# The first of three block pairs with eight plain d_ff tiles, and GpSimd's sums moved to VectorE

## The chip, the cores and the metric

The kernel runs on one core of one Trainium2 chip. Its time is the device time of one execution in microseconds. TensorE multiplies, VectorE, ScalarE and GpSimd work on elements, and SyncE here only sends transfers between the chip's outer memory (DRAM) and SBUF, the memory that the engines work in. Each engine runs its instructions in order. TensorE writes to PSUM, which has eight banks of 128 x 512 floats here. TensorE's clock has two levels, 1.2 and 2.4 GHz; the profile's column PEclk shows the mean share of the upper one that was granted.

## The reference

Attention with a memory (B = 4, H = 8, S = 576, D = 64) gives x, 2304 tokens of 512 numbers. A gated network follows, with d_ff = 1536:

```
g   = x @ w_gate                    # 2304 x 1536
u   = g * sigmoid(g) * (x @ w_val)
out = u @ w_out                     # 2304 x 512
```

The change concerns this second part alone. Weights come as 64-bit floats and are rebuilt as 32-bit ones on the chip.

## The kernel before, in words

**Precision.** A number is held as a high and a low part in TensorE's type; a product of two such numbers is three matmuls (high-high, high-low, low-high). Making the parts is a copy on ScalarE (the high one) and a subtraction on VectorE (the low one).

**Stages.** The attention runs first. Beside it d_ff tiles 0 to 3 (of twelve, 128 wide) are finished for tokens 0 to 1535, with their sums in the DRAM tensor `part`. x goes to the DRAM tensors `xdh` and `xdl`. Then comes the stage that the change is about, from line 693 on. It goes over three block pairs of 2 x 384 tokens in the order 1536, 0, 768 (`ORDER`): block pair 1 does all twelve tiles, pairs 2 and 3 do tiles 4 to 11 and add `part`.

**A unit** is one d_ff tile of one block pair. There are two ways to do its products with w_gate and w_val:

- *plain*, `eight` (L890): eight block products of the 2 x 2 split (2 token blocks, 2 halves of d_model, gate and value): 48 matmuls of 384 columns;
- *seven products*, `seven` (L918): a scheme with seven block products (`p1` to `p7`): 42 matmuls. It needs sums of weight blocks (`operands`, L744) and of x blocks (`fetch`, L788, and `sums`, L810), all of them split into parts again (`mixed`, L802, for x).

The gate goes through Silu on ScalarE, VectorE multiplies by the value (L909, L938), `halves` (L879) splits the result. The sums into d_model (`lower`, L858) are 18 matmuls of 512 columns for a unit; they stand between the products of the next unit. `inline` (L832) fixes this order on TensorE. The products use two PSUM banks in turn (`bank`, L886); the other six hold the output of a block pair.

Before, the first four units (tiles 0 to 3 of block pair 1) are plain and all others take seven products.

**Weights.** `weights2` (L708) converts one tile in three steps (gate, value, out), each with a load of 512 KB into one of two `wrawb` buffers (L711), L714 on ScalarE and L715, L721 and L722 on VectorE. Tiles 4 to 7 (`keep`) have buffers of their own, as plain floats for gate and value, from which `operands` makes both kinds of parts. Tiles 8 to 11 take over the buffers of tiles 0 to 3, as parts (`wsplit`); for them `operands` adds the parts together first, on GpSimd (L750). `convert` (L740) emits as many steps at each unit as `PACE` says: four at each of the first four, then one, then two. They go in the order of tiles 4 to 11.

**x.** `direct` (L798) loads parts of x from DRAM as they are (p1, p2, p4; for the plain units also p7). `fetch` loads the four blocks of a pair, the high parts into `xr` and the low parts, one after another, into the single buffer `xt`, and adds them on GpSimd (L795, 768 columns each). `sums` makes four sums of them on GpSimd (L804). `tokens` (L821) does both for the next block pair after the last unit of one.

**What sets the order.** Within an engine the order is fixed when the program is built: a planner takes instructions by a priority, which is the order of emission unless `later_by(n)` moves it n places back, and by times that it estimates. All loads of this stage go through SyncE's one queue.

Of the kernel before, what the change touches and what calls it, by code (L numbers as in the profile page):

```python
# [19 lines left out]
NPAIR = H // 2  # L20
# [25 lines left out]
PACE = (4, 4, 4, 4, 1, 1, 1, 1, 2, 2)  # L46
# [17 lines left out]
def attention_moe(ctx: ExitStack, tc: tile.TileContext, qt, kt_, v, m, beta, wg, wv, wo, out):  # L64
# [630 lines left out]
    with tc.tile_pool(name="w2", bufs=1, reuse_waits="tile") as w2, \  # L695
# [38 lines left out]
        def more():  # L734
            for f in later:
                yield from weights2(f)
# [51 lines left out]
        def fetch(t0):  # L788

            got = rot(mbp, "xr", [128, 4, 2, N2], F32, 1)  # L790
            for n, (i, j) in enumerate(((1, 0), (1, 1), (0, 0), (0, 1))):
                tmp = rot(mbp, "xt", [128, 2, N2], F32, 1)
                SP.dma_start(got[:, n], block(xdh, t0, i, j))
                SP.dma_start(tmp, block(xdl, t0, i, j))
                POOL.tensor_tensor(got[:, n], got[:, n], tmp, op=ALU.add)  # L795
            return got

        def direct(t0, p, i, j):  # L798
            for dst, src in zip(xs[p], (xdh, xdl)):
                SP.dma_start(dst.bitcast(F32), block(src, t0, i, j))  # L800

        def mixed(got, p, out, a, b, op):  # L802

            POOL.tensor_tensor(out, a, b, op=op)  # L804
# [5 lines left out]
        def sums(got, which):  # L810
            a21, a22, a11, a12 = (got[:, n] for n in range(4))
            if "p6" in which:
                s = rot(mbp, "xm", [128, 2, N2], F32, 1)
                s1 = rot(mbp, "xt", [128, 2, N2], F32, 1)
                mixed(got, "p5", s1, a21, a22, ALU.add)
                mixed(got, "p6", s, s1, a11, ALU.subtract)
                mixed(got, "p3", a12, a12, s, ALU.subtract)
            if "p7" in which:
                mixed(got, "p7", a11, a11, a21, ALU.subtract)

        def tokens(t0, got):  # L821
            direct(t0, "p1", 0, 0)
            direct(t0, "p2", 0, 1)
            direct(t0, "p4", 1, 1)
            sums(got, ("p6", "p7"))

        blocks = [(t0, later if t0 < NT1 else list(range(NF))) for t0 in ORDER]
# [62 lines left out]
        def eight(f, down):  # L890

            hi, lo = wsplit[f]
            u = []
            for i, at in enumerate((("p1", "p2"), ("p7", "p4"))):
                g = hold(("zg", "zh")[i])
                for gv in range(2):
                    ps = bank()
                    n = 0
                    for kk in range(NPAIR):
                        o = gv * 512 + (kk + 2 * gv) % 4 * 128  # L900
                        c = slice(o, o + 128)
                        xh, xl = (x[:, kk % 2, :] for x in xs[at[kk // 2]])
                        for wt, xx in ((hi, xh), (hi, xl), (lo, xh)):
                            inline(PE.matmul(ps[:, 0:N2], wt[:, c], xx, start=(n == 0), stop=(n == 11)))
                            n += 1
                    if gv == 0:
                        ACT.activation(g, ps[:, 0:N2], AF.Silu, scale=W_ONE)
                    else:
                        DVE.scalar_tensor_tensor(  # L909
                            out=g, in0=ps[:, 0:N2], scalar=W_ONE, in1=g, op0=ALU.mult, op1=ALU.mult  # L910
                        )
                        u.append(halves(i, g))
                    if down and (i or gv):
                        for _ in range(2):
                            down.pop(0)()
# [27 lines left out]
        for p, i, j in (("p1", 0, 0), ("p2", 0, 1), ("p7", 1, 0), ("p4", 1, 1)):  # L943
            direct(first, p, i, j)
        ready = {}
        last = None
        for n, unit in enumerate(units):
            t0, f, fs = unit
            whole = f not in keep and n < FC1
# [5 lines left out]
            if FC1 - 1 <= n < len(units) - 1:  # L955
                with later_by(LATE):
                    ready[n + 1] = operands(units[n + 1][1])
            if f == fs[-1] and t0 != blocks[-1][0]:
# [3 lines left out]
                lambda j=j, last=last: lower(*last, j) for j in (range(2 * nj) if n <= FC1 else TURN)  # L962
            ]
            last = (unit, eight(f, down) if whole else seven(ready.pop(n), down))
            if n == FC1 - 1:
                sums(got, ("p7",))
            if f == fs[len(fs) // 2] and t0 != blocks[-1][0]:
                got = fetch(blocks[[t for t, _ in blocks].index(t0) + 1][0])
            if f == fs[-1] and t0 != blocks[-1][0]:
                tokens(units[n + 1][0], got)  # L970
            if f == fs[1] and t0 == blocks[-1][0]:
                whole_x = got.rearrange("p n k c -> p (n k c)")
# [54 lines left out]
```

## Time and profile before

| | us |
|---|---|
| median of 3 runs | 759.21 |
| lowest and highest | 754.63, 762.9 |
| the profiled execution | 761.55 |
| its span, first to last instruction | 759.5 |
| start of the first plain unit in it | 370.93 |

The profile is of one execution. Its instructions are named by engine (PE is TensorE, DVE VectorE, ACT ScalarE, POOL GpSimd, SP SyncE; PEld the loading of weights into TensorE), by line, and by tile as output<-inputs. Times of the trace count from the first instruction. A row of busy time gives a stretch from:to, its length, then for PE, PEld, DVE, ACT and POOL the busy us and (x how many instructions), then PEclk, the share of time that the DMA engines were busy, and GB/s. A busy engine is one with an instruction under way, whatever that instruction itself waits for.

### The profile page before, as it was taken

Reading aid. Unit: us, or ns where it says so; the run is one execution under the profiler, and the core shown is the slowest. Engines: PE = TensorE matmul, PEld = TensorE weight load, DVE = VectorE, ACT = ScalarE, POOL = GpSimd, SP = SyncE. Lnnn points to the kernel's source line nnn. Section 1 sums busy time; section 2 is a strip of 40 time slices with the busy share of each in tenths; the row PEclk is TensorE's granted clock in tenths of the full one; section 3 lists DMA queues with packets and bytes.
Section 4 is the critical chain, followed back from the end, with each engine's and each line's share of the span. In section 5 each row is a group of like instructions: output and inputs, shape, how many; then the busy total and the mean of one; then the engine's idle time right before and its main releaser. Section 6 shows DMA issues by size and latency. Waiting matters only on the chain.

```text
span 759.5 us, 11605 instructions
## 1 busy us (share of the span) xinstructions
PE 685.0 (90%) x4028; PEld 603.8 (80%) x4028; DVE 559.2 (74%) x1298; ACT 416.7 (55%) x909; POOL 271.8 (36%) x288
## 2 busy tenths in 40 slices
PE   5798989999899998999889585979997999999998
PEld 3586769997798977988778574858986999989996
DVE  8999736867877778776469979996678765874544
ACT  6667538586666866757434353553473343643431
POOL 5998545443555435522014325112015320002100
PEclk9999899999899998999979897999999899999999
DMA  9455452303623124020484552320164000620002
GB/s 260 165 170 183 134 163 69 113 13 108 196 86 84 48 97 160 33 100 6 143 303 156 188 187 69 121 83 1 54 196 139 29 0 1 194 98 1 0 1 83
DMA packets 49562, 80.45 MB, mean 106 GB/s; under 512 B 12256, under 2 KB 30176, under 8 KB 49504
## 3 DMA queue, kind: packets, MB, share of 16 engines
q1 hardware_dynamic: 49360, 79.42, 32.4%
q8 instruction: 31, 0.51, 0.3%
q10 hardware_dynamic: 144, 0.29, 0.1%
q14 instruction: 27, 0.22, 0.1%
HBM read 62.40 MB, written 17.30 MB: 105 GB/s over the span
## 4 chain that ended last, share of the span: by engine, by line
PE 56%; DVE 23%; DMA 8%; issue 5%; ACT 5%; POOL 3%; SPq 0%; DVEq 0%; ACTq 0%; POOLq 0%
PE g L844 9%; PE m L844 9%; PE tr L865 5%; PE s L865 4%; PE g L207 4%; PE s L406 3%; PE m L207 3%; PE tr L483 3%; PE av L626 2%; PE av L865 2%; DMA wrawb<-in_wg_dram 2%; PE av L612 2%; DMA wrawb<-in_wv_dram 1%; PE m L216 1%; DVE wab L722 1%
## 5 line engine op out<-in xcount | busy, mean ns | idle before, releaser
L750 POOL TENSOR_TENSOR rb<-wh,wl 128x1024 f32<-128x1024 f32 x12 | 30.2, 2513 | 151.5 <-DVE tt L768 138.1
L770 DVE TENSOR_TENSOR tl<-tt,th 128x512 fp32r<-128x512 f32 x48 | 36.1, 752 | 40.7 <-ACT th L769 40.6
L795 POOL TENSOR_TENSOR xr<-xr,xt 128x768 f32<-128x768 f32 x12 | 23.1, 1929 | 117.4 <-DMA xt<-xdl 103.8
L769 ACT CAST th<-tt 128x512 fp32r<-128x512 f32 x48 | 29.8, 621 | 60.1 <-PE m L844 29.4
L420 ACT ACTIVATE pl<-pl,mx 128x384 f32<-128x384 f32 (+1 forms) x64 | 42.5, 666 | 26.0 <-DVE mx L416 25.9
L459 POOL TENSOR_SCALAR pl<-pl,rs 128x384 f32<-128x384 f32 (+1 forms) x64 | 45.7, 732 | 18.5 <-ACT x L510 12.2
L114 DVE TENSOR_TENSOR g2l<-tr,g2h 128x512 fp32r<-128x512 f32 (+1 forms) x66 | 36.6, 572 | 19.7 <-ACT g2h L465 19.1
L459 POOL TENSOR_SCALAR ps<-ps,rs 128x128 f32<-128x128 f32 (+1 forms) x64 | 28.2, 460 | 55.5 <-DVE rs L456 36.1
L483 PE MATMUL tr<-ident,pl 128*128 128x128 f32 x224 | 39.9, 310 | 6.6 <-POOL pl L459 4.2
L416 DVE CUSTOM_DVE_ANT_0 pl<-s,maskp 128x384 f32<-128x384 f32 (+1 forms) x56 | 33.0, 618 | 13.1 <-PE s L406 13.0
L406 PE MATMUL s<-kh,qh 64*128 64x128 f32 (+3 forms) x112 | 26.1, 443 | 15.9 <-DVE mx L416 9.1
L483 PEld LDWEIGHTS tr<-ident,pl 128*128 128x128 f32 x224 | 28.8, 158 | 13.1 <-POOL pl L459 7.6
L465 ACT CAST g2h<-tr 128x512 fp32r<-128x512 f32 (+1 forms) x66 | 31.0, 493 | 10.5 <-PE tr L483 9.9
L420 ACT ACTIVATE ps<-ps,mx 128x128 f32<-128x128 f32 (+1 forms) x64 | 28.8, 451 | 8.1 <-DVE mx L416 8.0
L406 PEld LDWEIGHTS s<-kh,qh 64*128 64x128 f32 x112 | 11.8, 198 | 24.7 <-DVE mx L416 10.8
L510 ACT COPY x<-av 64x256 f32<-64x256 f32 (+1 forms) x44 | 17.3, 394 | 25.1 <-PE av L626 15.3
L626 PE MATMUL av<-g2h,vs 128*128 128x320 f32 (+2 forms) x110 | 30.1, 289 | 0.1
L714 ACT ACTIVATE web<-wrawb 128x512 f32<-128x512 f32 x24 | 16.1, 673 | 24.6 <-DMA wrawb<-in_wg_dram 11.1
L626 PE MATMUL av<-g2l,vs 128*128 128x320 f32 (+2 forms) x110 | 29.4, 300 | 0.2
L511 DVE TENSOR_TENSOR x<-av,x 64x256 f32<-64x256 f32 (+1 forms) x44 | 19.9, 453 | 12.8 <-ACT x L510 12.2
L110 POOL TENSOR_SCALAR qh<-qr 128x640 fp32r<-128x640 f32 x16 | 12.7, 794 | 43.9 <-PE s L437 40.5
L882 ACT CAST uh<-zh 128x384 fp32r<-128x384 f32 x28 | 14.3, 512 | 23.8 <-DVE zh L938 12.5
(405 smaller groups left out, 2655.1 us busy)
## 6 DMA issues: line engine op xcount, KB each, us to landing
qr<-in_qt_dram SPq DMA_DIRECT2D x16, 384.0 KB, 4.0
xr<-xdh SPq DMA_DIRECT2D x12, 384.0 KB, 4.2
xt<-xdl SPq DMA_DIRECT2D x12, 384.0 KB, 4.2
kr<-in_kt_dram SPq DMA_DIRECT2D x15, 288.0 KB, 3.5
xdh<-xh SPq DMA_DIRECT2D x15, 288.0 KB, 2.4
xdl<-xl SPq DMA_DIRECT2D x15, 288.0 KB, 3.2
wrawb<-in_wg_dram SPq DMA_DIRECT2D x8, 512.0 KB, 3.7
wrawb<-in_wv_dram SPq DMA_DIRECT2D x8, 512.0 KB, 3.5
```

Source lines behind the costliest of these rows:

```text
L114: return eng.tensor_tensor(dst, src, hi.bitcast(F32), op=ALU.subtract)
L207: PE.matmul(ps, wt[:, c], xx[:, kk, :], start=(n == 0), stop=(n == 11))
L406: mm = PE.matmul(ps[h][:, 0:w], q[rows, t * 128 : t * 128 + 128], k[rows, 0:w], start=(i == 0), stop=(i == 2))
L416: read[id(ps[h])] = DVE.tensor_tensor_reduce(out=p[:, 0:w], in0=ps[h][:, 0:w], in1=maskp[:, 512 - w : 512], op0=ALU.add, op1=ALU.min, scal ...
L420: ACT.activation(p[:, 0:w], p[:, 0:w], AF.Exp, bias=mx[:, c + h : c + h + 1], scale=-1.0, accum_out=self.sm[:, c + h : c + h + 1],)
L459: POOL.tensor_scalar(p, p, rs[:, i : i + 1], 1.0, op0=ALU.mult, op1=ALU.mult)
L465: ACT.copy(view(g[0]), src)
L483: PE.transpose(tr[:, c * 128 : c * 128 + 128], p[:, (k0 + c) * 128 : (k0 + c) * 128 + 128], ident)
L626: PE.matmul(av[:, o:320], self.vs[:, h, kk, :], keys, start=(kk == 0 and g is self.g2[0]), stop=(kk == 4 and g is self.g2[1]),)
L770: DVE.tensor_tensor(tl[:, c], t[:, c], th[:, c].bitcast(F32), op=ALU.subtract)
L844: inline(PE.matmul(ps[:, 0:N2], wt[:, c], xx[:, kk, :], start=(start and n == 0), stop=(n == 5), skip_group_check=not start,))
L865: inline(PE.matmul(po[j], a[:, c], b, start=(f == fs[0] and n == 0), stop=(f == fs[-1] and n == 2)))
```

## The change

- In block pair 1 the tiles go in the order 0 to 3, 8 to 11, 4 to 7. The first eight are plain, the last four take seven products. The other pairs are as before.
- Tiles are converted in the order 4, 5, 8, 9, 10, 11, 6, 7 (`TURNS`), three steps (one tile) at each of the eight plain units.
- The sums that GpSimd made (L750 as two halves of 512 columns, L795, L804) are on VectorE.
- `mixed` is taken apart: `sums` makes all four sums of a pair at one place, `spread` splits one of them.
- `fetch` and `sums` for the next block pair are emitted at the fourth and third unit from a pair's end, behind by `LATE` = 60 places; for the first pair at units 1 and 2, with the splits at units 3, 4, 5 and 7.
- `direct` loads each half of a block's d_model (k) with a transfer of its own, and for the first pair in the order p1, p7, then p2 and p4 by k.
- In the first unit (`begin`) the four products are made together, half of d_model by half, with two of the output's banks beside the two of the ring, so that p1 and p7 come first. In the last plain unit (`back`) the second token block goes first.

The core of the diff:

```
-PACE = (4, 4, 4, 4, 1, 1, 1, 1, 2, 2)
+TURNS = (4, 5, 8, 9, 10, 11, 6, 7)
...
-                POOL.tensor_tensor(w, bh[:, 0:1024].bitcast(F32), bl[:, 0:1024].bitcast(F32), op=ALU.add)
+                for c in (slice(0, 512), slice(512, 1024)):
+                    DVE.tensor_tensor(w[:, c], bh[:, c].bitcast(F32), bl[:, c].bitcast(F32), op=ALU.add)
...
-                POOL.tensor_tensor(got[:, n], got[:, n], tmp, op=ALU.add)
+                DVE.tensor_tensor(got[:, n], got[:, n], tmp, op=ALU.add)
...
+        def direct(t0, p, i, j, ks=(0, 1)):
+            for k in ks:
+                for dst, src in zip(xs[p], (xdh, xdl)):
+                    SP.dma_start(dst[:, k].bitcast(F32), block(src, t0, i, j)[:, k])
...
+            DVE.tensor_tensor(s1, a21, a22, op=ALU.add)
+            DVE.tensor_tensor(s, s1, a11, op=ALU.subtract)
+            DVE.tensor_tensor(a12, a12, s, op=ALU.subtract)
+            DVE.tensor_tensor(a11, a11, a21, op=ALU.subtract)
+            return dict(p6=s, p7=a11, p5=s1, p3=a12)
+
+        def spread(mix, p):
             h, l = xs[p]
             for k in range(2):
-                ACT.copy(h[:, k], out[:, k])
-                DVE.tensor_tensor(l[:, k], out[:, k], h[:, k].bitcast(F32), op=ALU.subtract)
+                ACT.copy(h[:, k], mix[p][:, k])
+                DVE.tensor_tensor(l[:, k], mix[p][:, k], h[:, k].bitcast(F32), op=ALU.subtract)
...
+        whole = list(range(FC1)) + later[NF - 2 * FC1 :]
+        blocks = [(t0, later if t0 < NT1 else whole + later[: NF - 2 * FC1]) for t0 in ORDER]
...
+        def eight(f, down, begin, back):
...
+            if begin:
+                for ks in ((0, 1), (2,)):
+                    for i, gv in todo:
+                        run(i, gv, ks)
+            for i, gv in todo:
+                ps = run(i, gv, (3,) if begin else range(NPAIR))
...
+        direct(first, "p1", 0, 0)
+        direct(first, "p7", 1, 0)
+        for k in range(2):
+            direct(first, "p2", 0, 1, (k,))
+            direct(first, "p4", 1, 1, (k,))
...
             with later_by(LATE):
-                convert(PACE[n] if n < len(PACE) else 0)
-            if n == 1:
-                got = fetch(first)
-                sums(got, ("p6",))
+                if n < nw:
+                    convert(3)
+                if n == 1:
+                    got = fetch(first)
+                if n == 2:
+                    mix = sums(got)
+                if 3 <= n < 6:
+                    spread(mix, ("p6", "p5", "p3")[n - 3])
...
+            if n < nw:
+                last = (unit, eight(f, down, n == 0, n == nw - 1))
+            else:
+                last = (unit, seven(ready.pop(n), down))
+            if n == nw - 1:
+                spread(mix, "p7")
+            if not end:
+                follows = blocks[[t for t, _ in blocks].index(t0) + 1][0]
+                with later_by(LATE):
+                    if at == len(fs) - 4:
+                        got = fetch(follows)
+                    if at == len(fs) - 3:
+                        mix = sums(got)
+                if at == len(fs) - 1:
+                    tokens(follows, mix)
```

## Rows read from the trace of the kernel before

**Rows 1.** Page, part 1: busy us (share of the span) and instructions of each engine

```profile
PE 685.0 (90%) x4028; PEld 603.8 (80%) x4028; DVE 559.2 (74%) x1298; ACT 416.7 (55%) x909; POOL 271.8 (36%) x288
```

**Rows 2.** Busy time (length; PE, PEld, DVE, ACT, POOL; clock): units, then block pair 1

```profile
370.93:390.24 19.31, 13.95 (x61) 12.43 (x60) 6.02 (x13) 6.05 (x10) 0.00 (x0) 0.73 0.83 284
390.24:402.76 12.52, 12.52 (x68) 11.72 (x67) 11.68 (x20) 5.95 (x11) 4.07 (x2) 1.00 0.55 194
416.20:438.85 22.65, 14.61 (x67) 13.49 (x66) 20.03 (x31) 6.97 (x14) 8.05 (x4) 0.85 0.57 178
455.89:478.90 23.01, 14.70 (x61) 12.85 (x60) 21.55 (x28) 8.33 (x17) 10.73 (x6) 0.78 0.25 85
478.90:522.23 43.33, 37.06 (x181) 31.29 (x180) 40.97 (x76) 23.57 (x46) 7.72 (x3) 1.00 0.22 74
522.23:533.71 11.48, 11.48 (x61) 10.66 (x60) 6.35 (x14) 4.67 (x10) 2.60 (x1) 1.00 0.00 0
370.93:556.67 185.74, 153.64 (x738) 137.40 (x738) 148.51 (x250) 84.25 (x163) 44.40 (x21) 0.92 0.40 134
```

**Rows 3.** Busy time by stretch: block pair 2, its longest unit, block pair 3

```profile
556.67:657.38 100.71, 95.46 (x481) 87.61 (x480) 71.20 (x121) 47.46 (x96) 25.42 (x12) 0.97 0.25 76
580.63:599.98 19.35, 14.82 (x61) 13.09 (x60) 16.80 (x17) 5.37 (x12) 11.27 (x6) 0.82 0.13 41
657.38:751.11 93.73, 92.38 (x481) 84.92 (x479) 51.66 (x103) 37.00 (x74) 7.60 (x3) 1.00 0.11 38
```

**Rows 4.** TensorE in order of time: start, us, instruction, [idle before <-releaser]

```profile
426.48 0.69 PE L904 MATMUL g<-xbh,wh 128*128 128x384 f32 x1 [8.04 <-DVE zh L909]
```

**Rows 5.** VectorE in order of time, ahead of that L909

```profile
420.67 2.28 DVE L722 SCALAR_TENSOR_TENSOR wr<-wrawb,wr 128x512 int32<-128x512 int32 x1
422.88 0.41 DVE L715 TENSOR_SCALAR web<-web 128x512 f32<-128x512 f32 x1
...
424.13 0.69 DVE L722 SCALAR_TENSOR_TENSOR wr<-wrawb,wr 128x512 int32<-128x512 int32 x1
424.73 0.55 DVE L808 TENSOR_TENSOR xp5l<-xt,xp5h 128x384 fp32r<-128x384 f32 x1
425.20 0.42 DVE L760 TENSOR_TENSOR tt<-wr 128x256 f32<-128x256 f32 x1
```

**Rows 6.** GpSimd in order of time: the last of four sums in a row

```profile
420.29 2.11 POOL L804 TENSOR_TENSOR xr<-xr 128x768 f32<-128x768 f32 x1
```

**Rows 7.** L770 (ns min/median/max, first and last start); a wait of block pair 1 (us, times, longest)

```profile
L770 DVE TENSOR_TENSOR tl<-tt,th x48: 677/693/2310, 394.6 to 726.4; 128x512 fp32r<-128x512 f32 x48
...
DVE web L715 <- ACT web L714: 14.5, 9, 7.3
```

**Rows 8.** Page, part 5: GpSimd's L750 and L795, busy, mean ns | idle before, releaser

```profile
L750 POOL TENSOR_TENSOR rb<-wh,wl 128x1024 f32<-128x1024 f32 x12 | 30.2, 2513 | 151.5 <-DVE tt L768 138.1
...
L795 POOL TENSOR_TENSOR xr<-xr,xt 128x768 f32<-128x768 f32 x12 | 23.1, 1929 | 117.4 <-DMA xt<-xdl 103.8
```

**Rows 9.** SyncE in order of time, around the start of block pair 1

```profile
370.36 0.41 SPq L253 DMA_DIRECT2D part<-o  x1
...
376.87 0.32 SPq L640 DMA_DIRECT2D xdl<-xl  x1
377.29 0.40 SPq L800 DMA_DIRECT2D xp7h<-xdh  x1
```

**Rows 10.** TensorE in order of time, the first plain unit

```profile
380.91 0.66 PE L904 MATMUL m<-xp7h,wh 128*128 128x384 f32 x1 [3.56 <-DMA xp7h<-xdh]
...
382.64 0.52 PE L904 MATMUL m<-xp7h,wl 128*128 128x384 f32 x1
382.96 0.52 PE L904 MATMUL m<-xp7h,wh 128*128 128x384 f32 x1
```

**Rows 11.** Page, part 6: loads, KB each, median us from issue to landing

```profile
xt<-xdl SPq DMA_DIRECT2D x12, 384.0 KB, 4.2
...
wrawb<-in_wg_dram SPq DMA_DIRECT2D x8, 512.0 KB, 3.7
```

More of the change, by code (lines that the diff above doesn't have):

```diff
@@ L734, in more @@
         def more():
-            for f in later:
+            for f in TURNS:
                 yield from weights2(f)
@@ L888, in bank @@
             return ring[turn2[0] % 2]
-        def eight(f, down):
+        def eight(f, down, begin, back):
             hi, lo = wsplit[f]
[L893 to L915, printed above, removed]
@@ new lines, in eight, with run @@
+            u = [None, None]
+            todo = [(i, gv) for i in ((1, 0) if back else (0, 1)) for gv in range(2)]
+            held = {}
+            def run(i, gv, ks):
+                if (i, gv) not in held:
+                    held[(i, gv)] = po[2 * nj - 2 + gv] if begin and i else bank()
+                ps = held[(i, gv)]
+                for kk in ks:
+                    o = gv * 512 + (kk + 2 * gv) % 4 * 128
+                    c = slice(o, o + 128)
+                    at = (("p1", "p2"), ("p7", "p4"))[i][kk // 2]
+                    xh, xl = (x[:, kk % 2, :] for x in xs[at])
+                    for n, (wt, xx) in enumerate(((hi, xh), (hi, xl), (lo, xh))):
+                        inline(PE.matmul(
+                            ps[:, 0:N2], wt[:, c], xx, start=(kk == 0 and n == 0), stop=(kk == NPAIR - 1 and n == 2)
+                        ))
+                return ps[:, 0:N2]
@@ new lines, in eight @@
+            if begin:
[4 more added lines that the diff above has]
+                ps = run(i, gv, (3,) if begin else range(NPAIR))
+                if gv == 0:
+                    g = hold(("zg", "zh")[i])
+                    ACT.activation(g, ps, AF.Silu, scale=W_ONE)
+                else:
+                    DVE.scalar_tensor_tensor(out=g, in0=ps, scalar=W_ONE, in1=g, op0=ALU.mult, op1=ALU.mult)
+                    u[i] = halves(i, g)
+                if down and (i, gv) != todo[0]:
+                    for _ in range(2):
+                        down.pop(0)()
@@ L948, in attention_moe @@
             t0, f, fs = unit
[L949 removed]
+            at = fs.index(f)
+            end = t0 == blocks[-1][0]
             with later_by(LATE):
[L951 to L956 removed]
+                if n < nw:
[6 more added lines that the diff above has]
+                    spread(mix, ("p6", "p5", "p3")[n - 3])
+                if nw - 1 <= n < len(units) - 1:
                     ready[n + 1] = operands(units[n + 1][1])
[L958 removed]
+            if at == len(fs) - 1 and not end:
                 for j in TURN[0:nj]:
@@ L961, in attention_moe @@
             down = [] if last is None else [
-                lambda j=j, last=last: lower(*last, j) for j in (range(2 * nj) if n <= FC1 else TURN)
+                lambda j=j, last=last: lower(*last, j) for j in (range(2 * nj) if n <= nw else TURN)
             ]
[L964 to L972, printed above, removed]
+            if n < nw:
+                last = (unit, eight(f, down, n == 0, n == nw - 1))
+            else:
+                last = (unit, seven(ready.pop(n), down))
[10 more added lines that the diff above has]
+                    tokens(follows, mix)
+            if at == 1 and end:
+                whole_x = slots["xr"][1][0].rearrange("p n k c -> p (n k c)")
                 for j in range(2 * nj):
```

31 lines of the change are left out of this document (10 added, 21 removed).

## The prediction

> **What bounds the kernel now.** I read the page first, then the busy time unit by unit (a unit is one d_ff tile of one block pair, its products on TensorE and the sums into d_model of the unit before it), then single instructions where a unit is long. The page shows TensorE busy for 90% of the span and VectorE for 74%; GpSimd has 271.8 us [rows 1]. That average hides two regimes. In block pair 1 (from 370.93 us) a plain unit takes 12.52 us and a seven-product unit 11.48 us when TensorE never waits [rows 2]: the difference, 1.04 us, is six matmuls of 384 columns. Four plain and eight seven-product units need 4 x 12.52 + 8 x 11.48 = 141.9 us; the block took 185.74. In block pair 2, 8 x 11.48 = 91.84 stands against 100.71, in block pair 3 against 93.73 [rows 3]. So block 1 loses 43.8 us, block 2 8.9, block 3 1.9, and the product work itself is the floor.
>
> What ends the waits is read at the longest one. TensorE stands 8.04 us before a matmul that needs a PSUM bank which VectorE's L909 has to read [rows 4]. Ahead of L909 in VectorE's order stand instructions of 2.1 to 2.3 us; the same line, L722, takes 0.69 us a little later [rows 5]. The long ones stand while GpSimd runs its sums of the experts' inputs back to back, the last at 420.29 for 2.11 us, and the short ones begin when it is through [rows 6]. So here an engine that is off the critical path lengthens VectorE's instructions to its own two microseconds, by about 1.5 us each (2.28 instead of 0.69). Block 1 has 21 GpSimd operations [rows 2], so some 21 x 1.5 = 31 us of VectorE's 148.5 busy us are this lengthening; VectorE is busy for 80% of the block.
>
> **The change, part by part.** All durations are of the profiled run, from instructions that nothing lengthened: VectorE takes 0.42 us for 256 columns, 0.55 for 384, 0.42 for a one-operand 512 and 0.69 for L722 [rows 5], and 0.69 for 512 columns with two SBUF operands [rows 7].
>
> 1. *Plain products.* Units of tiles 8 to 11 in block 1 become plain: 4 x 1.04 = +4.2 us of TensorE. The floor of block 1 is 8 x 12.52 + 4 x 11.48 = 146.1 us, less what unit 0 doesn't have (below). Their operands (L750, then 3.1 us of VectorE each) fall away, and with them the chain conversion, GpSimd sum, VectorE sums that the late seven-product units waited for: three such units take 43.33 us, 3.0 us each above 11.48, with VectorE busy for 40.97 of them [rows 2].
>
> 2. *GpSimd's sums go to VectorE.* L750 (12 now, 8 after), L795 (12) and L804 (12) leave GpSimd [rows 8]. A 768-column add on VectorE isn't in the trace. It costs more than a 512-column one (0.69) and less than two of them (1.38); these three sizes rise by 0.14 per 128 columns, so I take 0.69 + 0.28 = 0.97 us. The two halves of L750 are 1.38 us. VectorE gets 24 x 0.97 + 8 x 1.38 = 34 us over the span, 15.5 of it in block 1 (the 16 adds of two fetches and their sums; all operands made there are of tiles 4 to 7), and loses about 31 us of lengthening in block 1 alone.
>
> 3. *Does VectorE then have room?* A plain unit's own work is 4 x 0.55 = 2.2 us. A tile's conversion is three times 0.42 + 0.42 + 0.69 and one or three subtractions of 0.69: 5.3 us (tiles 4 to 7) or 6.7 (8 to 11). With a fetch (3.9), sums (3.9), one expert's split (1.1) and operands (4.2) where they fall, units 0 to 7 hold 7.5, 11.4, 12.7, 10.0, 10.0, 10.0, 7.5, 12.7: 82 us against about 105 of products. A seven-product unit's own work is 7 x 0.55 = 3.9 us, operands 4.2 (4.4 with L750's halves). Units 8, 9 and 11 come to 11.9, 11.9 and 12.4 of 11.48, and so do four more at the later block boundaries; the others to some 8. In the rows, the instruction behind L722 starts 0.60 us after it, and L722 shows 0.69 [rows 5], so these sums are high by a tenth. VectorE has room, with seven tight units.
>
> 4. *The start.* Unit 0 takes 19.31 us now at a mean clock of 0.73 [rows 2]. SyncE, in order, sends p7's loads at 377.29, behind the last attention pair's store at 376.87 [rows 9]; the first product on p7 waits 3.56 us and then runs 0.52 us a matmul instead of 0.34 [rows 10]. The change asks for p7 before p2 and p4, and takes products as data come. At best p7 leaves in the queue's free time after 370.36 [rows 9], and only the last pair's columns are late: stored by about 379, loaded some 4 us later [rows 11], end near 383, so 12 us. At worst p7 again leaves at 377, now with 12 products to do before it and not 24, and 36 products follow at the lower of the two clock levels: 380.9 + 27 x 0.32 (the steps in [rows 10]) + 9 x 0.17 = 391, so 20 us. The order of SyncE's queue decides, which this trace can't show; I take 17, nearer the worst, since the queue now has p7 behind that store. The 20 DMA issues more that the split by k brings cost SyncE 0.4 us each, in a queue that is mostly free.
>
> 5. *Order of conversions.* Three per unit instead of four and then one; tiles 8 to 11 are ready two units ahead. Each unit needs three loads of 512 KB at 3.7 us [rows 11] in 12.5 us, through two buffers: covered, but the adds of a fetch share SyncE's queue and its one xt buffer. Where the conversion is late, L715 stands at the head of VectorE's queue and L909 behind it. I take 2 us for units 1 to 7 (bounds 0 and 10: now unit 1 loses nothing and unit 3, with GpSimd's sums inside, 10.1 [rows 2]).
>
> 6. *What remains as stall.* Units 8 to 11: 2 us; block 2: 2; block 3: 2 as now. Bounds: 0, and for each of the seven tight units the 3.0 us that the three crowded units lose [rows 2].
>
> **The sum.** Block 1: 17 + 7 x 12.52 + 2 + 4 x 11.48 + 2 = 154.6 instead of 185.7: -31.1. Block 2: 91.84 + 2 = 93.8 instead of 100.7: -6.9. Block 3 and the tail behind it: 0. Together -38.0 us. The profiled execution took 761.55 us (span 759.5), which gives 723.5; its time lies 2.3 us above the median of the runs, from which it gives 721.2. I say 722 us.
>
> **Rivals.**
> *VectorE becomes the bound.* The seven tight units each lose 3.0 us, 20.7 instead of the 6 that parts 3 and 6 allow: +15, so 737 us. For: their sums exceed 11.48 us, and a seven-product unit gives VectorE less time per bank than a plain one. Against: in block 2 as it is, most units run without a wait and VectorE has 29 us free [rows 3], and the background work may slide over a unit. The Trainium skill, page "Perfetto Trace Analysis", section "Optimizing Scalar/DVE Operations", speaks for this rival: with DVE saturated, offloading to GPSIMD may make sense, and the change does the opposite. By that sentence alone block 1 would grow by the 15.5 us moved; the same section doubts the offload between these two, because they share a read port, and the lengthened rows agree with the doubt.
>
> *Everything hides.* Unit 0 at 12 us, no stall but block 3's 1.9: 723.5 - 5 - 6 = 712.5, and 711 off the median.
>
> *The stalls are the loads', not GpSimd's.* VectorE waited 14.5 us for L714 in block 1, which waits for weight loads [rows 7], and some stalls come with GpSimd idle. If only the stalls of the three units with GpSimd's sums go (10.1, 11.5 and 7.9 us [rows 2, 3]) and 4.2 us of products are added: 761.5 - 29.5 + 4.2 = 736. If none go: 766, which is no change.
>
> *Slower: the adds stand at the head of VectorE's queue.* GpSimd spent 117.4 us idle before the 12 adds of L795, 103.8 of it for the landing of xt [rows 8]: 9.8 us each. GpSimd held up nobody by that. VectorE runs in order, and an add that waits there holds L909, L928 and every split behind it; TensorE is covered, by the products between two uses of a PSUM bank, for 1.04 us and one sum into d_model, (11.48 - 7 x 1.04) / 6 = 0.70, in a seven-product unit and for twice that in a plain one: 1.7 to 3.5, say 2.5 us. If VectorE waited as long: 12 x (9.8 - 2.5) = +88, so about 811 us. It decides from (761.5 - 723.5) / 12 + 2.5 = 5.7 us of waiting per add. Against: xt lands 4.2 us after its issue [rows 11], the adds are now set late in the unit, and most of GpSimd's wait was for its next work, not for a late load; L715, which waits on a load in the same way, cost VectorE 14.5 us over 24, 7.3 of it once, before any add [rows 7].
>
> **How the numbers follow.** Forecast 0.60 (712 to 732), all hides 0.13, VectorE bound 0.18, loads 0.06 (half of it no change), adds at the head 0.03. Range 709 to 742: below lies part of the second case, above some of the third, the 766 and the 811. A change within 1% (7.6 us) is about what can't be told from no change here, with runs from 754.63 to 762.9. Faster by more than that: 0.60 + 0.13 + 0.18 + 0.03 = 0.94; same 0.03; slower 0.03.
>
> **What would show it.** Right: no VectorE instruction of these forms above 0.8 us after 371 us; eight plain units near 12.5 us; 768-column adds near 0.97 us; block 2's unit of 19.35 us gone; TensorE's idle time in block 1 under 15 us, most of it in unit 0. Wrong: VectorE waits of several us for xt in front of L909 or its successor; units 8, 9 and 11 above 14 us; SyncE's queue held by the single xt buffer while L714 waits; or a start of unit 1 later than 391 us.

## The result and the profile after

The change took the median from 759.4 us (754.63 to 762.9, 4 runs) to 725.5 us (723.74 to 727.18, 4 runs); the ratio is 0.956, with an interval of 0.950 to 0.961. The profiled execution of after took 723.74 us, with a span of 721.9. Of all executions behind the numbers below one was disturbed: it is the profiled one of the kernel with the old start, 1630.29 us with TensorE busy for 99% of it, and neither that kernel's ratio nor any reading of a trace uses it.

The page of after, part 1, against [rows 1]:

```profile
PE 671.8 (93%) x4052; PEld 596.4 (83%) x4052; DVE 532.0 (74%) x1302; ACT 405.4 (56%) x889; POOL 193.4 (27%) x252
```

VectorE took over GpSimd's sums (32 are left of 36, in 40 instructions) and is busy for 27 us less. Part of the 27 us is work that fell away with the sums for four units (3.1 us each by part 1 of the prediction); how much the move itself shortened the other instructions is read below, from a kernel in which only the sums moved. Busy time of after by stretch, columns as in [rows 2]: unit 0, units 1 to 7, units 8 to 11, the eight plain units together, block pair 1, block pair 2, its longest unit, block pair 3:

```profile
367.79:388.39 20.60, 13.62 (x60) 12.24 (x59) 3.86 (x9) 4.47 (x8) 0.00 (x0) 0.75 0.73 244
388.39:476.44 88.05, 88.02 (x463) 82.11 (x463) 76.43 (x148) 41.97 (x82) 0.00 (x0) 1.00 0.55 175
476.44:524.23 47.79, 46.80 (x241) 42.45 (x240) 37.85 (x75) 26.71 (x54) 0.00 (x0) 1.00 0.26 83
...
367.79:476.44 108.65, 101.64 (x523) 94.35 (x522) 80.29 (x156) 46.44 (x89) 0.00 (x0) 0.95 0.58 189
...
367.79:524.23 156.44, 148.44 (x762) 136.80 (x762) 118.14 (x231) 73.15 (x142) 0.00 (x0) 0.97 0.49 156
524.23:620.05 95.82, 92.72 (x481) 84.95 (x480) 69.78 (x138) 47.67 (x96) 0.00 (x0) 1.00 0.27 83
536.01:551.10 15.09, 12.02 (x61) 10.53 (x60) 12.06 (x22) 5.91 (x12) 0.00 (x0) 1.00 0.56 183
620.05:713.51 93.46, 92.24 (x481) 84.93 (x479) 54.94 (x109) 36.69 (x74) 0.00 (x0) 1.00 0.11 36
```

Units 1 to 7 need 7 x 12.52 = 87.64 us and took 88.05: the stalls of the middle of block pair 1 are gone. GpSimd does nothing in the whole stage. What is left above the floor stands at four places: unit 0 (20.6 us, clock 0.75), units 8 to 11 (1.9 us over 45.9), block pair 2 (4.0 over 91.84) and block pair 3 (1.6).

After's VectorE lines, first L722 between 371 and 620 us (ns min/median/max, first and last start), then groups of the page's part 5, against [rows 5] and [rows 8]:

```profile
L722 DVE SCALAR_TENSOR_TENSOR wab<-wrawb,wab x16: 681/688/695, 396.7 to 485.4; 128x512 int32<-128x512 int32 x16
L722 DVE SCALAR_TENSOR_TENSOR wr<-wrawb,wr x8: 681/685/691, 386.0 to 478.3; 128x512 int32<-128x512 int32 x8
...
L796 DVE TENSOR_TENSOR xr<-xr,xt 128x768 f32<-128x768 f32 x12 | 11.5, 955 | 5.6 <-DMA xt<-xdl 5.0 <-DMA xr<-xdh 0.6
L751 DVE TENSOR_TENSOR rb<-wh,wl 128x512 f32<-128x512 f32 x16 | 11.0, 685 | 0.0
```

L722 varies by 14 ns, where it went up to 2.28 us before. An add of 768 columns takes 0.955 us on VectorE; it took 1.93 on GpSimd.

**Where the 37.6 us of span come from** (759.5 to 721.9): block pair 1 gave 29.3 (185.74 to 156.44), block pair 2 4.9 (100.71 to 95.82), block pair 3 0.3. The remaining 3.1 lie ahead of the stage: the first plain product started at 367.79 instead of 370.93. No line of the attention is changed, and in the profiled runs of eight kernels that share it this start lies between 367.8 and 373.0. I count it as variation between runs, not as an effect of the change; no run shows that directly. By the medians, 759.4 and 725.5, the gain is 33.9 us.

**The start** is the place that came out worst. After, SyncE's queue and TensorE in order of time:

```profile
373.91 0.32 SPq L640 DMA_DIRECT2D xdl<-xl  x1
374.32 0.40 SPq L802 DMA_DIRECT2D xp7h<-xdh  x1
```

```profile
371.09 0.28 PE L626 MATMUL av<-g2l,vs 128*128 128x64 f32 x1
377.09 0.69 PE L910 MATMUL s<-xp7h,wh 128*128 128x384 f32 x1 [5.72 <-DMA xp7h<-xdh]
379.50 0.69 PE L910 MATMUL s<-xp7h,wh 128*128 128x384 f32 x1 [0.91 <-DMA xp7h<-xdh]
...
384.34 0.52 PE L910 MATMUL g<-xbh,wl 128*128 128x384 f32 x1
384.66 0.42 PE L910 MATMUL s<-xp4h,wh 128*128 128x384 f32 x1
384.92 0.34 PE L910 MATMUL s<-xp4l,wh 128*128 128x384 f32 x1
```

p7 is asked for ahead of p2 and p4 in the program, but leaves the queue right behind the attention's last store, as in [rows 9]. TensorE has only p1's 12 products before it, stands 5.72 us, and then runs at the lower of its two levels (0.52 us a matmul, 1.2 GHz) until 384.66; from 384.92 on it is 0.34 us again (2.4 GHz).

### The profile page after: what moved, and what is told of

Same layout as the page of the kernel before. It is cut to its first block, busy times and chain, and to the rows that moved or that the text cites. A ratio compares the mean times of both kernels' runs of the same rounds, so it can differ in the third digit from the quotient of the medians.

```text
span 721.9 us, 11594 instructions
## 1 busy us (share of the span) xinstructions
PE 671.8 (93%) x4052; PEld 596.4 (83%) x4052; DVE 532.0 (74%) x1302; ACT 405.4 (56%) x889; POOL 193.4 (27%) x252
## 4 chain that ended last, share of the span: by engine, by line
PE 53%; DVE 20%; DMA 12%; ACT 5%; issue 5%; POOL 3%; SPq 1%; DVEq 0%; ACTq 0%; POOLq 0%
PE g L847 9%; PE m L847 9%; PE tr L868 5%; PE g L207 4%; PE s L868 4%; PE s L406 3%; PE m L207 3%; PE av L626 3%; PE tr L483 3%; DMA wrawb<-in_wo_dram 2%; DMA xt<-xdl 2%; PE av L868 2%; DMA wrawb<-in_wg_dram 2%; DMA wrawb<-in_wv_dram 2%; PE m L216 1%
## 5 line engine op out<-in xcount | busy, mean ns | idle before, releaser
L770 ACT CAST th<-tt 128x512 fp32r<-128x512 f32 x40 | 24.9, 621 | 52.8 <-PE g L847 26.1
L771 DVE TENSOR_TENSOR tl<-tt,th 128x512 fp32r<-128x512 f32 x40 | 27.6, 690 | 32.0 <-ACT th L770 32.0
L459 POOL TENSOR_SCALAR ps<-ps,rs 128x128 f32<-128x128 f32 (+1 forms) x64 | 28.2, 459 | 58.7 <-DVE rs L456 37.6
L378 PE MATMUL tr<-mm,ph 128*128 128x130 f32 x160 | 24.9, 292 | 0.1
L715 DVE TENSOR_SCALAR web<-web 128x512 f32<-128x512 f32 x24 | 10.2, 424 | 20.0 <-ACT web L714 20.0
L114 POOL TENSOR_TENSOR ql<-qr,qh 128x640 fp32r<-128x640 f32 x15 | 24.8, 1654 | 0.1
L612 PE MATMUL av<-g,vz 128*128 128x320 f32 (+2 forms) x100 | 23.0, 380 | 0.6 <-ACT g L330 0.6
```

Source lines behind the costliest of these rows:

```text
L114: return eng.tensor_tensor(dst, src, hi.bitcast(F32), op=ALU.subtract)
L459: POOL.tensor_scalar(p, p, rs[:, i : i + 1], 1.0, op0=ALU.mult, op1=ALU.mult)
L771: DVE.tensor_tensor(tl[:, c], t[:, c], th[:, c].bitcast(F32), op=ALU.subtract)
```

## The experiments

### The two halves of the change apart

The change has two large parts that can be had alone: which engine makes the sums, and the order (eight plain units, conversions beside them, the new start). The first two kernels are the missing corners of the square.

New order, sums of weights and of x back on GpSimd:

```
-                    DVE.tensor_tensor(w[:, c], bh[:, c].bitcast(F32), bl[:, c].bitcast(F32), op=ALU.add)
+                POOL.tensor_tensor(w, bh[:, 0:1024].bitcast(F32), bl[:, 0:1024].bitcast(F32), op=ALU.add)
...
-                DVE.tensor_tensor(got[:, n], got[:, n], tmp, op=ALU.add)
+                POOL.tensor_tensor(got[:, n], got[:, n], tmp, op=ALU.add)
...
-            DVE.tensor_tensor(s1, a21, a22, op=ALU.add)
+            POOL.tensor_tensor(s1, a21, a22, op=ALU.add)
```

> The changed kernel with the 32 sums (operand sums, adds of a fetch, sums of a pair) back on GpSimd; all else as changed. My theory (GpSimd's sums lengthen VectorE's instructions by about 1.5 us each, and that was most of the loss): VectorE's instructions that meet a sum show 1.5 to 2.8 us again, the units that hold the four sums of a pair lose 8 to 11 us each, about 750 us. Rival (what helped is the order: eight plain units and conversions two units ahead): 726 us, within 3 of the changed kernel.

Old order, sums on VectorE:

```
-                POOL.tensor_tensor(w, bh[:, 0:1024].bitcast(F32), bl[:, 0:1024].bitcast(F32), op=ALU.add)
+                for c in (slice(0, 512), slice(512, 1024)):
+                    DVE.tensor_tensor(w[:, c], bh[:, c].bitcast(F32), bl[:, c].bitcast(F32), op=ALU.add)
...
-                POOL.tensor_tensor(got[:, n], got[:, n], tmp, op=ALU.add)
+                DVE.tensor_tensor(got[:, n], got[:, n], tmp, op=ALU.add)
...
-            POOL.tensor_tensor(out, a, b, op=op)
+            DVE.tensor_tensor(out, a, b, op=op)
```

> The kernel before with the same sums moved to VectorE and nothing else. My theory: the three units with GpSimd's sums (10.1, 11.5 and 7.9 us lost) come down to 2 or 3 us each, but VectorE has 138 us of work in block pair 1 against 142 of products, so its crowded units stay: 728 to 738 us. Rival (the order helped): at least 750 us, since the late conversions and the operand sums for tiles 8 to 11 stay.

| order | sums on | median, us | ratio to before | block pair 1 | block pair 2 |
|---|---|---|---|---|---|
| old | GpSimd (before) | 759.4 | 1 | 185.7 | 100.7 |
| old | VectorE | 736.65 | 0.969 (0.964 to 0.975) | 167.1 | 99.5 |
| new | GpSimd | 744.95 | 0.982 (0.975 to 0.989) | 171.0 | 101.0 |
| new | VectorE (after) | 725.5 | 0.956 (0.950 to 0.961) | 156.4 | 95.8 |

Each ratio is to before on the same chip, which is not the same for all kernels; differences are therefore taken from ratios, on 759.4 us. The sums alone are worth 23 us, the order alone 14 (8 to 19 by its interval), both 34: nearly the sum of the two. So neither expectation was right about the new order with sums on GpSimd: 744.95 us lies between the 750 of the theory and the 726 of the rival, and the order counts too. Which of its parts gives those 14 us, the plain units or the conversions, no run separates; for the new start see below. The row of the new order with sums on GpSimd, block pair 1:

```profile
368.30:539.30 171.00, 151.13 (x763) 138.21 (x762) 125.79 (x213) 73.78 (x142) 35.57 (x17) 0.95 0.43 143
```

The rows of the old order with the sums on VectorE, block pair 1 and L722:

```profile
368.87:535.97 167.10, 150.17 (x738) 134.02 (x738) 137.03 (x276) 84.17 (x163) 0.00 (x0) 0.96 0.45 149
```

```profile
L722 DVE SCALAR_TENSOR_TENSOR wr<-wrawb,wr x8: 680/684/693, 386.0 to 439.6; 128x512 int32<-128x512 int32 x8
```

VectorE has 26 instructions more in this block than before (276 against 250) and is busy for 11.5 us less (137.0 against 148.5). The 26 are of 0.69 to 0.95 us, 18 to 25 us together; so what the others lost in length is 29 to 36 us. In the other corner, new order with sums on GpSimd, the long instructions are back. VectorE there, in order of time, while GpSimd makes four sums in a row:

```profile
416.55 2.22 DVE L722 SCALAR_TENSOR_TENSOR wab<-wrawb,wab 128x512 int32<-128x512 int32 x1
418.69 2.03 DVE L715 TENSOR_SCALAR web<-web 128x512 f32<-128x512 f32 x1
420.63 2.15 DVE L818 TENSOR_TENSOR xp5l<-xt,xp5h 128x384 fp32r<-128x384 f32 x1
```

The same kernel, GpSimd in order of time:

```profile
416.31 1.91 POOL L808 TENSOR_TENSOR xt<-xr 128x768 f32<-128x768 f32 x1
418.30 2.13 POOL L809 TENSOR_TENSOR xm<-xt,xr 128x768 f32<-128x768 f32 x1
420.51 1.87 POOL L810 TENSOR_TENSOR xr<-xr,xm 128x768 f32<-128x768 f32 x1
```

Each of the three VectorE instructions ends within 0.6 us of a GpSimd one and has about its length. L715, with one operand, is lengthened like the others (0.41 us in [rows 5]). The unit around them takes 21.7 us.

### GpSimd's sums as such, or waiting for them?

In that comparison the sums also change who waits for whom. So after was given GpSimd work that nobody waits for (VectorE's instructions stand in the same order in both traces): six adds of 128x512 on a tile that nothing reads any more, in each plain unit.

```
+            if n < nw:
+                for m in range(6):
+                    idle = POOL.tensor_tensor(maskp, maskp, maskp, op=ALU.add)
+                    if m == 0:
+                        follow(idle, chain[0], "in the next unit", mybir.DependencyClass.Sync)
```

> The changed kernel with six more GpSimd instructions for each of the eight plain units, 128x512 adds of a tile that nobody reads any more; VectorE's order is unchanged and nothing waits for them. My theory: VectorE's instructions that meet one are lengthened by one GpSimd instruction (some 1.4 us by the 1.9 of 768 columns), the plain units become VectorE-bound, at least +15 us, 740 us or more. Rival (GpSimd cost time only by being waited for): 726 us, VectorE's durations unchanged.

And the same with sixteen writes of zeros, which take GpSimd longer but read nothing:

```
-                for m in range(6):
-                    idle = POOL.tensor_tensor(maskp, maskp, maskp, op=ALU.add)
+                for m in range(16):
+                    idle = POOL.memset(maskp, 0.0)
```

> The same place with 16 GpSimd memsets of that tile (128x512, 0.53 us each by the one at the kernel's start), which write SBUF and read nothing: GpSimd is about as busy as with the adds. If what lengthens VectorE is GpSimd's reading of SBUF, instructions of VectorE with two SBUF inputs keep 0.42 to 0.69 us and the time stays near 726 us; if any GpSimd work does it, as with the adds, 740 us or more.

Each of the two kernels ran once. With the adds: 756.3 us, beside 762.36 for before on the same chip (after, by its ratio, would be 729). With the writes of zeros: 729.15. Busy time over the eight plain units, GpSimd's group on the page, and L722 (ns min/median/max); the kernel with adds first:

```profile
369.77:505.55 135.78, 110.67 (x523) 99.93 (x523) 108.62 (x157) 47.42 (x89) 56.12 (x42) 0.91 0.47 154
...
L992 POOL TENSOR_TENSOR maskp<-maskp 128x512 f32<-128x512 f32 x48 | 64.1, 1336 | 88.9 <-PE s L868 57.8
...
L722 DVE SCALAR_TENSOR_TENSOR wr<-wrawb,wr x8: 681/876/1524, 387.9 to 506.4; 128x512 int32<-128x512 int32 x8
```

The kernel with writes of zeros, the same and then L721:

```profile
368.45:478.99 110.54, 101.38 (x523) 93.54 (x523) 84.45 (x156) 45.89 (x88) 65.05 (x112) 0.97 0.56 185
...
L992 POOL MEMSET maskp<- 128x512 f32 x128 | 74.1, 579 | 55.2 <-PE s L910 28.0
...
L722 DVE SCALAR_TENSOR_TENSOR wab<-wrawb,wab x16: 674/688/694, 397.6 to 489.8; 128x512 int32<-128x512 int32 x16
...
L721 DVE TENSOR_SCALAR wab<-web x16: 415/624/824, 395.9 to 487.5; 128x512 int32<-128x512 int32 x16
```

The reader can set three rows side by side: after, adds, zeros. VectorE's 156 or 157 instructions of these units are busy for 80.3, 108.6 and 84.5 us; the stretch takes 108.7, 135.8 and 110.5. So 42 adds on GpSimd, for which nobody waits, cost 27 us, and 112 writes of zeros, with more GpSimd time, cost 2. It is what GpSimd reads that lengthens VectorE's instructions with two operands in SBUF; L925, which has one of its two in PSUM, stays at 0.54 to 0.56 us beside the adds. The instructions with one operand (L721) are lengthened beside the adds as well, up to 1.27 us from 0.42, and they feel the writes too, by 0.2 us in the median on `wab`.

The Trainium skill, page "SBUF — State Buffer", section "Who interferes with whom", states this: a VectorE instruction with two SBUF inputs contends with a GpSimd instruction that reads SBUF, not with one that only writes it, and `tensor_scalar` can contend through another mode. Both halves of that agree with the rows here (L722 stays at 0.69 us beside writes and goes up to 1.52 beside reads; L721 goes from 0.42 to 0.62 in the median beside writes).

### The start

Three kernels go at unit 0. One leaves after's start out: the old order of loads (still each in two halves), products of the first unit block by block.

```
-        direct(first, "p7", 1, 0)
-        for k in range(2):
-            direct(first, "p2", 0, 1, (k,))
-            direct(first, "p4", 1, 1, (k,))
+        for p, i, j in (("p1", 0, 0), ("p2", 0, 1), ("p7", 1, 0), ("p4", 1, 1)):
+            direct(first, p, i, j)
...
-                last = (unit, eight(f, down, n == 0, n == nw - 1))
+                last = (unit, eight(f, down, False, n == nw - 1))
```

> The changed kernel with its first unit done as the others (loads p1, p2, p7, p4, products bank by bank), which undoes that part of the change alone. If the new start gained what it is made for, the first unit takes longer than 20.6 us here, 728 us or more; by the traces so far it gained nothing: 19.3 us as before the change, 724 us; same within 1 us if the end is set by the last load.

726.2 us, 0.955 (0.952 to 0.959): no difference from after. The new start gained nothing that can be measured; how long unit 0 takes without it no trace shows.

The second gives p7 the buffer that p2 has, which is free early, so that p7 can be loaded ahead of the attention's end:

```
-        xs = {p: [... for part in "hl"] for p in ("p6", "p7", "p5", "p4", "p3")}
-        xs["p2"] = [x[:, 2:4, :] for x in xb]
+        xs = {p: [... for part in "hl"] for p in ("p6", "p2", "p5", "p4", "p3")}
+        xs["p7"] = [x[:, 2:4, :] for x in xb]
```

> The changed kernel with the rooms of p7 and p2 exchanged: p7 lies where p2 lay, in the tile that is free early, p2 in the new pool. Theory (the first plain unit is late because p7's loads leave SyncE's queue behind the last pair's store, so TensorE has 12 products to do and then waits 5.7 us): p7's loads leave before that store, 24 products stand before the wait, 24 behind it, the first plain unit takes 17 us and not 20.6: 722 us. Rival (the unit ends with the last loads and the clock's lower level, whatever is done before): 20 us again, 725.5 us.

727.64 us, 0.956 (0.952 to 0.961): no gain. TensorE's two waits of this unit 0:

```profile
384.15 0.69 PE L910 MATMUL m<-xp2h,wh 128*128 128x384 f32 x1 [5.50 <-DMA xp2h<-xdh]
394.03 0.44 PE L910 MATMUL m<-xbh,wh 128*128 128x384 f32 x1 [2.62 <-ACT zg L923]
```

The wait for p7 is gone and stands before p2 now. With p1 and p7 there early, the 24 products took their place on TensorE ahead of the attention's last ones, so the last store came 7.7 us after the first product (380.67 behind 372.99), where after has 5.6 (373.38 behind 367.79). Every load behind that store moved back with it. So the third orders the first plain product behind the attention's last:

```
-                            PE.matmul(
+                            self.last = PE.matmul(
...
-            if chain[0] is not None:
-                follow(mm, chain[0], "products and sums take turns")
+            if chain[0] is None:
+                chain[0] = pairs[-1].last
+            follow(mm, chain[0], "products and sums take turns")
```

It was tried on top of the next section's kernel, alone and then with the exchange of buffers.

### Block pair 2

After's longest unit of block pair 2 (15.09 us in place of 11.48) waits for VectorE. TensorE's longest wait there, then VectorE ahead of it:

```profile
549.25 0.44 PE L847 MATMUL g<-xp3h,bh 128*128 128x384 f32 x1 [1.81 <-DVE zv L946]
```

```profile
543.45 0.96 DVE L796 TENSOR_TENSOR xr<-xr,xt 128x768 f32<-128x768 f32 x1 [2.03 <-DMA xt<-xdl]
544.44 0.96 DVE L809 TENSOR_TENSOR xt<-xr 128x768 f32<-128x768 f32 x1
545.43 0.96 DVE L810 TENSOR_TENSOR xm<-xt,xr 128x768 f32<-128x768 f32 x1
...
546.91 0.95 DVE L811 TENSOR_TENSOR xr<-xr,xm 128x768 f32<-128x768 f32 x1
547.78 0.95 DVE L812 TENSOR_TENSOR xr<-xr 128x768 f32<-128x768 f32 x1
548.65 0.55 DVE L946 TENSOR_TENSOR zv<-g,zv 128x384 f32<-128x384 f32 x1
```

The last add waits 2.03 us for its load, and all sums of the pair follow it in a row, some 5 us with hardly another instruction between, while L946, for which TensorE's bank waits, is behind them. The program asks for these adds at unit 4 of block pair 2 and for the sums at unit 5; the planner put both into unit 1; that it did so because their data could be there is an argument, not a reading. The kernel with the old order and the sums on VectorE has the same burst, here the add, and TensorE's wait behind the sums that follow it:

```profile
557.42 0.96 DVE L796 TENSOR_TENSOR xr<-xr,xt 128x768 f32<-128x768 f32 x1 [2.23 <-DMA xt<-xdl]
...
563.23 0.64 PE L845 MATMUL g<-xp3h,bh 128*128 128x384 f32 x1 [2.01 <-DVE zv L933]
```

The edit asks for one add in each of the units 1 to 4 and holds each, and the first sum of every pair, behind the products of its unit:

```
+                add = DVE.tensor_tensor(got[:, n], got[:, n], tmp, op=ALU.add)
+                if len(ns) == 1:
+                    follow(add, chain[0], "one add in a unit", mybir.DependencyClass.Sync)
...
+            one = DVE.tensor_tensor(s1, a21, a22, op=ALU.add)
+            follow(one, chain[0], "not before its unit", mybir.DependencyClass.Sync)
...
-                    if at == len(fs) - 4:
+                    if len(fs) > 8 and at == len(fs) - 4:
                         got = fetch(follows)
+                    if len(fs) == 8 and 1 <= at < 5:
+                        got = fetch(follows, (at - 1,))
```

> The changed kernel with the adds of block pair 3's x held to one in a unit of pair 2, and a pair's first sum held behind the products of its unit. Theory (the 3.6 us that the second unit of pair 2 loses are seven 768-column instructions in 6.1 us at the head of VectorE's queue, which the planner set early because they were ready): that unit comes to 11.5 to 12 us, no other loses over 1 us, 722 us. Rival (VectorE has too much work there wherever it stands): the loss moves to a later unit, 725.5 us.

719.87 us, 0.948 (0.944 to 0.951). Block pair 2 in it:

```profile
527.52:619.35 91.83, 91.83 (x481) 85.21 (x480) 69.86 (x138) 47.39 (x96) 0.00 (x0) 1.00 0.27 87
```

Eight units at the floor, with TensorE busy throughout and the same 69.9 us on VectorE: it was the place of the work, not its amount.

### The start again, and block pair 1 by units

On top of that, the first product behind the attention's last one:

> The kernel with one add in a unit, and TensorE's first plain product set behind the attention's last product. Theory (the first unit ends with the last pair's chain: its last products, store, load, and the twelve p1 products that TensorE does first only push that chain back by 2 us): the last store leaves 2 us earlier against the attention, the first unit ends 2 us earlier, 718 us. Rival (those products cost the chain nothing, its inputs come late anyway): 720 us as without it, or above.

723.2 us, 0.950 (0.946 to 0.954): no gain over 0.948. The store now leaves 2.2 us after the first product (376.32 behind 374.13), but p7's loads are still behind it, and TensorE waits 3.38 us for them. And with p7 in the buffer that is free early:

> The same with p7 in the room of p2. Theory: now 24 products stand behind the attention's last one and beside its store and the loads of p2 and p4; from the last store to the start of the second unit it takes 10 us and not 14, about 714 us. Rival (the earlier p7 gives the time back at the end of the unit, where ScalarE's Silu stands behind a conversion that waits for its load, 2.6 us when p7 alone was moved): 718 us.

720.25 us, 0.947 (0.943 to 0.951): no gain either, although unit 0 is far shorter. This kernel's unit 0, its units 3 and 4, and its block pair 1:

```profile
369.55:381.90 12.35, 9.92 (x52) 8.12 (x50) 1.50 (x4) 2.71 (x5) 0.00 (x0) 1.00 0.70 225
407.04:438.86 31.82, 26.39 (x133) 23.17 (x132) 26.72 (x52) 14.35 (x27) 0.00 (x0) 1.00 0.55 173
369.55:524.18 154.63, 145.79 (x753) 132.43 (x752) 119.16 (x230) 73.42 (x141) 0.00 (x0) 1.00 0.48 155
```

Unit 0 went from 20.6 to 12.35 us at full clock. Units 3 and 4 gave 6.8 us back (31.82 in place of 2 x 12.52); in after they lost 0.3. TensorE's two longer waits there, then VectorE ahead of the first:

```profile
411.36 0.44 PE L915 MATMUL g<-xbh,wh 128*128 128x384 f32 x1 [2.07 <-DVE zh L930]
...
427.94 0.45 PE L915 MATMUL g<-xbh,wh 128*128 128x384 f32 x1 [2.20 <-ACT wh L730]
```

```profile
409.01 0.95 DVE L815 TENSOR_TENSOR xr<-xr,xm 128x768 f32<-128x768 f32 x1
409.88 0.95 DVE L816 TENSOR_TENSOR xr<-xr 128x768 f32<-128x768 f32 x1
410.75 0.55 DVE L930 SCALAR_TENSOR_TENSOR zh<-g,zh 128x384 f32<-128x384 f32 x1
```

The picture of block pair 2 again, now with block pair 1's own sums for which after still had the slack of a long unit 0. One theory was that these sums are in the way, the other that the conversion is late whatever stands beside it. The last kernel asks for block pair 1's adds one per unit too, and for the sums in unit 4:

```
-                if n == 1:
-                    got = fetch(first)
-                if n == 2:
-                    mix = sums(got)
-                if 3 <= n < 6:
-                    spread(mix, ("p6", "p5", "p3")[n - 3])
+                if 1 <= n < 5:
+                    got = fetch(first, (n - 1,))
+                if n == 4:
+                    mix = sums(got)
+                if n == 5:
+                    spread(mix, "p6")
+                if n == 6:
+                    spread(mix, "p5")
+                    spread(mix, "p3")
```

> Base is e9_after_attention_p7_in_xb (ratio 0.9468, block pair 1 units 3 and 4 at 15.98 and 15.85 us). Block 1's own four adds are asked for one per unit, in units 1 to 4, each behind its unit's products, the sums in unit 4, the splits in units 5 and 6. Theory A (the seven us lost in units 3 and 4 come from the adds and sums standing in a burst ahead of the conversion in VectorE's order): units 3 and 4 back to about 12.5 us, -6 us against e9, about 714 us, ratio 0.939; what units 5 to 8 get in addition is small. Theory B (the conversion itself is late, since its loads start only at 376.5 us behind the loads of x, and the adds only show it): the loss moves to other units, time as e9 within 2 us, ratio 0.947. Theory C: the later adds make unit 8 or 9 wait for their operands: 722 us or more, with unit 8 above 15 us.

716.24 us (713.07 to 719.46), 0.9445 (0.941 to 0.948). Units 3 and 4, block pair 1, block pair 2:

```profile
411.95:437.00 25.05, 25.05 (x134) 23.45 (x133) 22.66 (x42) 12.07 (x24) 0.00 (x0) 1.00 0.51 162
373.44:521.86 148.42, 145.34 (x754) 134.26 (x753) 117.72 (x230) 73.73 (x141) 0.00 (x0) 0.99 0.51 161
521.86:613.69 91.83, 91.83 (x482) 85.23 (x480) 69.90 (x138) 47.37 (x96) 0.00 (x0) 1.00 0.28 86
```

Units 3 and 4 are at 12.52 us, and of the others only unit 0 has grown, by 1.0 us (13.37, at a clock of 0.87 instead of 1.00): the sums were in the way, the conversion was in time. Block pair 1 takes 148.4 us, 2.3 above the floor of 146.1. It is the trace that decides here, with 154.6 to 148.4 in this block, and not the time: the medians differ by 4 us, but between two chips; by the ratios it is 2 us, and the intervals of the last two kernels overlap. How much of the 6 us reaches the whole time is open. In the two profiled executions the stage also begins at different times (369.55 and 373.44), so that the spans differ by 2.2 us only. This version is the best one found, 8 to 9 us below after.

## Why the prediction was right, and where it was not

The forecast was 722 us with a range of 709 to 742; 725.5 was measured. The mechanism held. Some of its terms did not. (What the prediction calls an expert is one of the seven products.)

- **The lengthening** (what bounds the kernel, and part 2): right in cause and size. Estimated at 31 us of VectorE's time in block pair 1; the old order with the sums on VectorE shows 29 to 36, and the experiment with idle adds shows that GpSimd's reading causes it without anybody waiting. The 768-column add was put at 0.97 us and took 0.955.
- **VectorE has room** (part 3): right. Units 0 to 7 were put at 82 us of VectorE and took 80.3. Units 8 to 11 took 37.9, within their 45.9 of products. The rival in which VectorE becomes the bound fell: of the units called tight, 8 ran 13.28 us, 9 and 11 ran 11.55 and 11.48. The four later ones, which the prediction counts but doesn't name, lost little in block pair 2: of the 4.0 us there 3.6 are those of its second unit. The Trainium skill, page "Perfetto Trace Analysis", section "Optimizing Scalar/DVE Operations", says that offloading from a saturated VectorE to GpSimd may make sense, and doubts it for these two engines because of their shared read port. It is the doubt that the runs bear out: with VectorE busy for 80% of the block, moving the 36 sums the other way, from GpSimd to VectorE, made the kernel 23 us faster.
- **The start** (part 4): the term that was mis-sized. I took 17 us "nearer the worst", with 12 and 20 as bounds; it measured 20.6. The mechanism of the upper bound, p7 again behind the store, is what happened. What I missed is that asking for p7 earlier in the program doesn't bring it forward: what goes into that buffer leaves behind the last store. The two kernels with the exchanged buffer show it from the other side: there p7 is loaded before, and p2 leaves behind the store (381.61 behind 381.20 in the first of them).
- **Stalls of units 1 to 7** (part 5): 2 us estimated, 0.4 measured. **Units 8 to 11** (part 6): 2 estimated, 1.9 measured.
- **Block pair 2** (part 6 and the sum): -6.9 predicted, -4.9 measured, and the step is wrong in its cause. I put its loss down to GpSimd's sums at the unit of 19.35 us, with 2 us left over. With the sums on VectorE and the old order the block still takes 99.5 us: the lengthening had given way to a burst of the same sums in VectorE's queue (the add that waits 2.23 us for its load, four sums behind it, and TensorE's 2.01 us for L933). The loss ended only when the adds were spread over the units.
- **The sum**: block pair 1 came 1.8 us short, block pair 2 2.0, and the 3.1 us of the earlier attention end covered nearly all of it, so that -38.0 against -37.6 of span is luck, a better match than the steps deserve. The profiled execution before lay above its median and the one after was the shortest of its four; the medians show the difference: 725.5, not 722.
- **The rivals**: "the stalls are the loads'" (736 to 766) fell: its 766 because the sums alone were worth 23 us, its 736 because 725.5 was measured. It wasn't empty, though. With the old order and the sums on VectorE, block pair 1 still stands 25 us above its floor of 141.9, some of it in unit 0, and the new order took 11 us more off the time; whether it was by earlier conversions or by operands that fell away is open. "The adds stand at the head of VectorE's queue" was right in kind and wrong by far in price: the twelve adds waited 5.6 us in all, 0.5 each, where I had put the point from which it decides at 5.7 each; it did show as the 3.6 us of one unit. "Everything hides" (711; its own terms, 712.5 less 2.3, give 710.2) is what the best version came within some 5 us of, 716.24, by pacing the sums and mending the start.

## What to carry to other kernels

An instruction that suddenly takes two to five times its usual length, and ends when one of another engine does, isn't waiting for data: look for what the two engines share, and price the moved work against the lengthening that it ends, not against the idle engine's free time. When work moves to the engine on the critical path, spread it by hand, one piece for each use of the tight buffer; a planner that places it when its data are there makes a burst. Where a stall is mended, look for the next stage's slack that it had provided: here 8 us taken from unit 0 came back as 6.8 in units 3 and 4 until the sums there were paced too.

## What the runs showed of the hardware that was not expected

- GpSimd pays as well: its idle add of 128x512 took 1.04 us at the least, 1.24 in the median and once 5.04 (from 420.97; VectorE's instructions beside that one kept their usual lengths until 425.50, so either engine can be the one that is held up), and its write of zeros 0.52 to 1.15 us.
- A writing GpSimd isn't free for VectorE: one-operand instructions of 512 columns went from 0.42 to a median of 0.62 us (L721 on `wab`). No time was lost by it here beyond 2 us.
- The granted clock of unit 0 was 0.75 after a stand of 5.72 us, 1.00 in the kernel whose waits there were 1.37, 0.25 and 0.64 us, and 0.87 in the last kernel with 1.36, 0.64 and 0.28. So waits of nearly the same lengths went with different clocks; the runs don't settle what decides.
